# Attention and routed experts on one core: two score rounds for three, weight rows in pairs, a new static order, and a conditional end

## The chip, the cores and the metric

One core of one Trainium2 chip runs the program. The metric is device time in microseconds (us) of one execution; the program reads its inputs from HBM and leaves one output tensor there. Engines are named as in the profile: PE is the matrix engine, PEld its weight loads, DVE the vector engine, ACT the scalar engine, POOL is GpSimd, SP issues transfers.

## The reference

Two layers follow each other. The first is causal attention with a window of 128 positions and a linear distance bias, for 8 batches, 8 heads, 576 positions and a head width of 64. The second sends its 4608 rows of 512 features through a dense two-layer network, and each row also through one of 8 experts of the same size, chosen by the largest gate logit and weighted by its probability.

```python
scores = scale * np.matmul(q, k.transpose(0, 1, 3, 2))
mask = (rel >= 0) & (rel < window)
scores = np.where(mask, scores + bias[None], -1000000000.0)
attn = np.exp(scores - np.max(scores, axis=-1, keepdims=True)); attn = attn / (np.sum(attn, axis=-1, keepdims=True) + 1e-09)
x = np.matmul(attn, v)            # rows of 512: 8 heads side by side
y_dense = np.maximum(x @ w1_dense, 0.0) @ w2_dense
expert_idx = np.argmax(x @ w_gate, axis=1)
y_moe[mask] = gate_w[mask, None] * (np.maximum(x[mask] @ w1[e], 0.0) @ w2[e])
out = y_dense + y_moe
```

The inputs are one fixed draw. Worked out from the reference, the experts get 520, 553, 517, 462, 688, 634, 658 and 576 rows, which is 5, 5, 5, 4, 6, 5, 6 and 5 blocks of 128: 41 blocks.

## The kernel before, in words

The work is cut into 16 units: a batch with four of its eight heads. For a unit, q and k arrive as 128 partitions of 18 rows (`load_qk`), are turned in 32x32 squares by DVE (`turn`, L175), and rounded and put in position order by a copy (`round_qk`, L184), on ACT but for the first q. Scores are made transposed, keys on partitions, in three rounds `pr`, of key blocks (0, 1), (2, 3) and (4): `biases` writes the distance bias into four PSUM banks by 16 matmuls of 32x32 (L404), `scores` adds 16, 16 and 8 matmuls (L422), `expo` takes the exponential of two heads at a time on ACT (L435), `low` makes the low half of the probabilities on DVE (L446; the high half is every second bf16 of the float). The third round has 64 queries, so that its tiles are 128x128 where the others are 128x1024 elements. `attend` multiplies with v (L478) into one PSUM tile of two banks that is freed by `norm` (L496, L497). The result goes to POOL for a row buffer (`row_copy`, L510), and is turned by PE (`flip`, L525) for the gate and the dense layers.

For each batch the gate logits come out of `gate_a`, `gate_av` (DVE adds the two units, L570, L572) and `gate_b` (five matmuls in float, each two instructions, L579); DVE picks the expert (`gate_bv`, L590 to L601), PE counts rows per expert (`gate_c`, L613, which waits for L601), and DVE makes the slot of each row. POOL scatters x rows and dense results into two HBM buffers, ordered by expert (`send_x` L662, `send_y` L750). Weights come in by cast transfers that POOL issues (`load_weights`, L91).

The experts run on blocks of 128 slots. Fifteen whole blocks are taken after five batches (early blocks); the other blocks, always 28 for a total of 43, wait until all rows are scattered (`fetch` L1094 to L1115). A block is four transposes (`turn_x`, L1121), 16 matmuls of 128x128 (`layer1`, L1156), four of 128x512 (`layer2`, L1175), copies by ACT and DVE, and an indirect transfer to the output by POOL (`send_out`, L1199). Rows past an expert's last one are filled by 16 transfers that SP issues near the end, with addresses read from a table (`late_fill`, L1072). Blocks that hold no row then write nothing.

The order of the work on PE, ACT, DVE and SP is written out by hand in three lists of words: `FIRST` (batch 0), `CYCLE` (each of the next batches, `@1` and `@2` being work of one and two batches before) and `LAST` (batch 7 and early blocks). POOL has an order of its own, by `in_turn`. The blocks after the list run in a loop at the end.

Of the kernel before, what the change touches and what calls it, by code (L numbers as in the profile page):

```python
# [23 lines left out]
def kernel(  # L24
# [37 lines left out]
    NL = NB - NE  # L62
    RB = 32
# [108 lines left out]
    def turn(u, nm):  # L172
        t = raw.pop((nm, u))
        s = stg.tile([P, 2, S], F32, name=f"{nm}s", tag=f"{nm}s")
        nc.vector.transpose(out=s.rearrange("p c (r x) -> p r c x", r=R), in_=t)  # L175
        tmp[(nm, u)] = s

    def round_qk(u, nm, copy=nc.scalar.copy):
# [3 lines left out]
        else:  # L182
            d = kTs[u % 2]
        copy(  # L184
            out=d[:, :, 0:S].rearrange("p c (x r) -> p c r x", r=R),
            in_=s.rearrange("p c (r x) -> p c r x", r=R),
# [14 lines left out]
    load_q(0, nc.scalar)  # L201
# [33 lines left out]
    def mask_consts():  # L235
# [11 lines left out]
        for g in range(1, 4):  # L247
            nc.tensor.matmul(
                out=turned[g],
                lhsT=ident2[:, P - 32 * g : 2 * P - 32 * g],  # L250
                rhs=dist,
                start=True,
                stop=True,
            )
# [9 lines left out]
    def mask_rest():  # L264
        for h in range(4, H):
            mask_head(h)

    def more_constants():
        ut_f = ident_x["ut_f"]
        nc.vector.tensor_copy(out=ut_b, in_=ut_f)  # L270
        nc.vector.memset(ones_b, 1.0)

        nc.vector.memset(sel, 0.0)
        for h in range(2):
            nc.vector.tensor_reduce(
                out=sel[64 * h : 64 * h + 64, h, :],
                in_=ident_f.rearrange("p (c x) -> p x c", c=4)[
                    64 * h : 64 * h + 64, 0:E, :
                ],
                op=ALU.add,  # L280
                axis=AX.X,
            )
        for i in range(NT):
            nc.vector.tensor_scalar_add(
                out=tok_c[:, i : i + 1], in0=pidx_f, scalar1=float(i * P)
            )
        nc.vector.tensor_copy(out=em8, in_=em8_i)
        nc.vector.memset(em8[TAIL:P, NT - 1, :], 0.0)
        nc.vector.tensor_copy(out=em8x, in_=em8)
        nc.vector.memset(em8x[TAIL:P, NT - 1, :], 1.0)  # L290
        for i in range(2):
            nc.vector.memset(ohs[i][:, NT, :], 0.0)
        nc.vector.tensor_copy(out=base0, in_=base_i)
        nc.vector.tensor_copy(out=basee, in_=base_i)
        nc.vector.tensor_scalar_mul(out=row_f, in0=pidx_f, scalar1=float(P))
        nc.vector.memset(fill_x, 0.0)
        nc.vector.tensor_copy(out=fill_x.bitcast(I32)[:, TC : TC + 1], in_=oob_f)
# [3 lines left out]
    sel = consts.tile([P, 2, E], F32, name="sel")  # L301
# [14 lines left out]
    def pool_constants():  # L316
# [14 lines left out]
        nc.gpsimd.iota(base_i, pattern=[[ST, E]], base=0, channel_multiplier=0)  # L331
# [13 lines left out]
    def wg_load():  # L345
        nc.sync.dma_start(
            out=wg_pad[:, :, 0:E], in_=moe_w_gate.rearrange("(ds p) e -> p ds e", p=P)
        )
# [22 lines left out]
    lt = dbuf.tile([P, SP_ - DT[1][0] * P], F32, name="ltsb")  # L371
# [11 lines left out]
    def shape(pr):  # L383
        kjs = KP[pr]
        wid = PW if len(kjs) == 2 else TAIL
        return kjs, wid, wid * len(kjs)

    def biases(u, pr):
        hq = u % HQ
        _, _, tot = shape(pr)  # L390
# [957 lines left out]
```

## Time and profile before

| | us |
|---|---|
| median of 3 runs | 369.23 |
| lowest and highest | 366.98 and 371.61 |
| the profiled execution, its own time | 369.47 |
| its span, first to last instruction | 367.8 |
| outside its span | 1.7 |

The profile was taken on one execution. Its rows give, for groups of instructions, the busy time, the mean of one instruction in ns, and the idle time of the engine just before, with what ended it. Matmul ends are modelled, so that a single matmul's mean is longer than its share of the engine; sums over a chain of them are better for that.

### The profile page before, as it was taken

The numbers are of one execution on the slowest core, as the hardware profiler recorded it, in microseconds if no ns is written. First come the engines' busy times: TensorE is split into PE (matmuls) and PEld (weight loads), VectorE is DVE, ScalarE is ACT, GpSimd is POOL, SyncE is SP. The second block draws the span as 40 slices with busy tenths as digits, with TensorE's granted clock in tenths as the row PEclk, the third lists the DMA queues.
The fourth block names the chain that finished last, engine by engine and source line by source line (L and its number), as shares of the span: only waits on it lengthen the run. The fifth ranks groups of instructions, "written<-read, shape, count | busy, mean of one in ns | idle before, by whom it ended". The sixth has DMA issues, their size and how long they took to land.

```text
span 367.8 us, 12624 instructions
## 1 busy us (share of the span) xinstructions
PE 318.5 (87%) x4972; PEld 226.9 (62%) x5003; DVE 273.5 (74%) x487; ACT 272.1 (74%) x430; POOL 223.4 (61%) x245
## 2 busy tenths in 40 slices
PE   3385888987999999999898798999999699999990
PEld 0274565665756756766665675776766467777760
DVE  7867999878799898797996978763645446676660
ACT  5778689897899999799989879876555336555640
POOL 5027612774486786488578768557777535656552
PEclk9999899998999999899999899999999879999997
DMA  7859999289569969949939995798589999989730
GB/s 199 252 132 196 187 237 234 71 234 289 141 138 276 286 131 256 262 109 303 248 107 238 242 260 129 221 255 295 169 303 317 337 303 316 316 279 307 257 123 8
DMA packets 76731, 82.43 MB, mean 224 GB/s; under 512 B 43519, under 2 KB 61311, under 8 KB 76672
## 3 DMA queue, kind: packets, MB, share of 16 engines
q1 hardware_dynamic: 58704, 47.32, 44.7%
q0 software_dynamic: 17680, 33.12, 35.7%
q10 hardware_dynamic: 288, 1.18, 0.9%
q8 instruction: 40, 0.66, 0.8%
q14 instruction: 19, 0.16, 0.1%
HBM read 64.20 MB, written 28.66 MB: 253 GB/s over the span
## 4 chain that ended last, share of the span: by engine, by line
PE 19%; POOL 14%; issue 12%; DVE 9%; ACT 2%; POOLq 1%; DMA 0%; DVEq 0%
POOL out_dram L1199 10%; DVE plo L446 4%; PE yp L733 3%; PE ax L478 3%; PE hp L706 3%; PE hpm L1156 3%; PE y L1175 2%; POOL ys_dram L750 1%; DVE xf L497 1%; POOL xs_dram L662 1%; PE tp L525 1%; DVE qs L175 1%; POOL xrow L510 1%; DVE ks L175 1%; PE xps L1121 1%
## 5 line engine op out<-in xcount | busy, mean ns | idle before, releaser
L446 DVE TENSOR_TENSOR plo<-p 128x1024 bf16<-128x1024 f32 (+1 forms) x96 | 87.1, 929 | 3.6 <-ACT p L435 3.6
L435 ACT ACTIVATE p<-sq 128x1024 f32<-128x1024 f32 (+1 forms) x96 | 74.4, 792 | 9.3 <-PE sq L422 6.8
L478 PEld LDWEIGHTS <-p 128*128 128x128 bf16 (+1 forms) x1152 | 61.9, 105 | 16.3 <-DVE xf L497 8.6
L1199 POOL DMA_INDIRECT out_dram<-yo,xr x43 | 48.4, 1125 | 37.1 <-DVE yo L1187 33.1
L510 POOL CAST xrow<-xf 128x512 bf16<-128x512 f32 (+1 forms) x48 | 47.2, 987 | 38.7 <-DVE xf L497 31.1
L478 PE MATMUL ax<-vf,p 128*128 128x65 bf16 (+1 forms) x576 | 65.2, 203 | 4.6 <-DVE xf L497 4.5
L478 PE MATMUL ax<-vf,plo 128*128 128x65 bf16 (+1 forms) x576 | 64.5, 200 | 1.1 <-DVE plo L446 1.1
L478 PE MATMUL ax<-vl,p 128*128 128x64 bf16 (+1 forms) x576 | 64.7, 199 | 0.0
L662 POOL DMA_INDIRECT xs_dram<-xrow,slot x40 | 46.0, 1150 | 29.1 <-issue 21.3
L750 POOL DMA_INDIRECT ys_dram<-yt,slot x40 | 52.5, 1313 | 15.1 <-ACT yt L745 5.4
L478 PEld LDWEIGHTS <-plo 128*128 128x128 bf16 (+1 forms) x576 | 57.7, 105 | 1.4 <-DVE plo L446 1.3
L1187 DVE SCALAR_TENSOR_TENSOR yo<-y,xr,yr 128x512 f32<-128x512 f32 x43 | 32.1, 750 | 29.1 <-PE y L1175 28.4
L1156 PE MATMUL hpm<-xTm,ws 128*128 128x128 bf16 x688 | 45.7, 221 | 1.1 <-issue 1.0
L1175 PE MATMUL y<-w_all,hTm 128*128 x156 | 43.1, 389 | 0.9
L1156 PEld LDWEIGHTS <-ws 128*128 128x128 bf16 x688 | 41.3, 99 | 3.5 <-issue 1.9
L1168 ACT ACTIVATE hTm<-hpm 128x512 bf16<-128x512 f32 x43 | 25.7, 597 | 23.7 <-PE hpm L1156 22.0
L706 PE MATMUL hp<-xTb,w_all 128*128 128x256 bf16 (+1 forms) x256 | 40.9, 289 | 1.3 <-ACT hTd L721 1.2
L733 PE MATMUL yp<-w_all,hTd 128*128 128x512 bf16 (+1 forms) x145 | 39.0, 381 | 0.7
L184 ACT CAST kT<-ks 128x1152 fp32r<-128x1152 f32 x16 | 37.9, 2370 | 1.9 <-DVE ks L175 1.8
L1130 ACT COPY xTm<-xps 128x512 bf16<-128x512 bf16 x43 | 25.1, 587 | 18.4 <-PE xps L1121 18.3
L1145 DVE COPY ws<-w_all 128x2048 bf16 x43 | 30.1, 703 | 11.3 <-PE hpm L1156 6.5
L497 DVE TENSOR_TENSOR xf<-ax,recip 128x512 f32<-128x512 f32 (+1 forms) x48 | 28.8, 600 | 12.5 <-POOL xrow L510 8.4
(126 smaller groups left out, 538.5 us busy)
## 6 DMA issues: line engine op xcount, KB each, us to landing
yr<-ys_dram SPq DMA_DIRECT2D x43, 256.0 KB
kraw<-in_k_dram SPq DMA_DIRECT2D x16, 576.0 KB
vf<-in_v_dram SPq DMA_DIRECT2D x64, 128.0 KB
w_all<-in_moe_w_dram POOLq DMA_DIRECT2D x16, 512.0 KB, 8.1
qraw<-in_q_dram SPq DMA_DIRECT2D x14, 576.0 KB
xr<-xs_dram SPq DMA_DIRECT2D x43, 130.0 KB
ys_dram<-fill_x SPq DMA_DIRECT2D x8, 256.0 KB
qraw<-in_q_dram ACTq DMA_DIRECT2D x2, 576.0 KB
```

What stands on the lines that cost most here:

```text
L184: copy(out=d[:, :, 0:S].rearrange("p c (x r) -> p c r x", r=R), in_=s.rearrange("p c (r x) -> p c r x", r=R),)
L435: nc.scalar.activation(out=p32, in_=sqs[(u, pr)][i][:, :, 0:tot], func=ACT.Exp, scale=SCALE)
L446: nc.vector.tensor_tensor(out=plo, in0=p32, in1=phi, op=ALU.subtract)
L478: nc.tensor.matmul(out=ax[:rows, i, o0 : o0 + w], lhsT=lhs, rhs=rhs, start=(n == 1), stop=(n == 3 * len(kl)),)
L510: ins = nc.gpsimd.tensor_copy(out=xrows[b % 2].bitcast(BF16)[:rows, qis[0] : qis[0] + nt, hq * 256 : hq * 256 + 256], in_=cur[("xf", u, pr ...
L662: ins = nc.gpsimd.indirect_dma_start(out=xs_dram[:, :], out_offset=bass.IndirectOffsetOnAxis(ap=slots[b][:rows, t : t + 1], axis=0), in_=x ...
L706: nc.tensor.matmul(out=hp[:, 0 : c1 - c0], lhsT=w_all[:, E, 0, kc, c * P : c * P + P], rhs=cur[("xTb", b)][:, kc, c0:c1], start=(kc == 0), ...
L733: nc.tensor.matmul(out=yp[:rows, :], lhsT=cur[("hT", b, hf)][:, c, t0 * P : t0 * P + rows], rhs=w_all[:, E, 1, c, :], start=(c == 0), stop ...
L750: ins = nc.gpsimd.indirect_dma_start(out=ys_dram[:, :], out_offset=bass.IndirectOffsetOnAxis(ap=slots[b][:rows, t : t + 1], axis=0), in_=c ...
L1156: nc.tensor.matmul(out=hp[:, c, :], lhsT=ws[:, kc, c * P : (c + 1) * P], rhs=xT[:, kc, :], start=(kc == 0), stop=(kc == 3),)
L1175: nc.tensor.matmul(out=y, lhsT=hT[:, c, :], rhs=w_all[:, bass.DynSlice(er, 1), 1, c, :], start=(c == 0), stop=(c == 3),)
L1199: ins = nc.gpsimd.indirect_dma_start(out=out[:, :], out_offset=bass.IndirectOffsetOnAxis(ap=xr.bitcast(I32)[:, TC : TC + 1], axis=0), in_= ...
```

## The change

- Scores: two rounds of key blocks (0, 1) and (2, 3, 4). The 64 columns of block 4 take the unused part of block 3's bank, so every round is 128x1024. The last 64 queries of two heads are handled together (`attend_tail`, 18 matmuls where there were 24), in the second half of the PSUM tile of queries 256 to 511, whose `norm` takes the reciprocals of both.
- Turning: DVE's squares are written with two neighbouring rows interleaved, and the copy after it reads in order and writes pairs, where it read single elements 128 bytes apart. The first q is copied by ACT, and loaded by SP.
- Weights: row 256c + 2p + l lies at partition p, so that a partition takes two rows of HBM in one piece. `pick` takes every second column when x or inner features are turned or multiplied.
- Gate: four row blocks side by side (`gate_a` has 10 matmuls), `gate_b` has two matmuls for five, and the first unit's copy is done by ACT.
- Constants of the routing move from DVE to POOL; `xf` has three buffers for two.
- Routing: each expert's region begins with 128 filler rows, written at batch 0 by two transfers (`unused_rows`); `late_fill` goes. Late blocks are counted back from an expert's last row, so that the first of them can overlap an early one; the output transfer of block 15 waits for those of blocks 0 to 14.
- 41 blocks run always; the last two only if more than 26 late blocks are in use, by a register and a branch at the end.
- `FIRST`, `CYCLE` and `LAST` are all new. In `CYCLE`, 4 words stood between `gb` (choice of the expert, DVE) and `pc` (count, PE), none of them PE's; now 23 stand there, 5 of them PE's (`hp` three times, `mask`, `qk`). In `LAST`, `out:12` stands just before `out:15`.

```diff
+    NO = 41
+    def pick(t, c):
+        return t.rearrange("p (c x l) -> p c l x", x=P, l=2)[:, c // 2, c % 2, :]
...
-            out=w_all[:, e, wi, :, :],
-            in_=src.rearrange("(ks p) f -> p ks f", p=P),
+            out=w_all[:, e, wi, :, :].rearrange("p (c l) f -> p c (l f)", l=2),
+            in_=src.rearrange("(c p l) f -> p c (l f)", p=P, l=2),
...
-        nc.vector.transpose(out=s.rearrange("p c (r x) -> p r c x", r=R), in_=t)
+        nc.vector.transpose(
+            out=s.rearrange("p c (a x l) -> p a l c x", x=32, l=2),
+            in_=t.rearrange("p (a l) c x -> p a l c x", l=2),
+        )
...
-            out=d[:, :, 0:S].rearrange("p c (x r) -> p c x r", r=R),
-            in_=s.rearrange("p c (r x) -> p c x r", r=R),
+            out=d[:, :, 0:S].rearrange("p c (x a l) -> p c a x l", x=32, l=2),
+            in_=s.rearrange("p c (a x l) -> p c a x l", x=32, l=2),
...
-    load_q(0, nc.scalar)
+    load_q(0, nc.sync)
...
+    KK = [(0, 1), (2, 3, 4)]
+    def part(kj, odd):
+        c0 = {0: 0, 1: PW, 2: 0, 3: PW, 4: PW + P + TAIL}[kj]
+        if odd and kj >= 2:
+            c0 = 0 if kj == 4 else c0 + TAIL
+        return c0, min(PW, S - kj * P)
...
     def gate_a(u):
+        for t, c in [(t, c) for c in range(2) for t in range(4)] + [(4, 0), (4, 1)]:
+            r0, c0, w = 32 * (t % 4), t // 4 * P, min(P, S - t * P)
...
     def gate_av(u):
+        for r, c0, w in ((P, 0, P), (32, P, TAIL)):
+            src, dst = lp[0:r, c0 : c0 + w], lt[0:r, c0 : c0 + w]
+            if u % HQ == 0:
+                nc.scalar.copy(out=dst, in_=src)
+            else:
+                nc.vector.tensor_tensor(out=dst, in0=dst, in1=src, op=ALU.add)
...
-        for t in range(NT):
+        for t0, t1 in ((0, 4), (4, NT)):
...
-                lhsT=w_all[:, E, 0, kc, c * P : c * P + P],
+                lhsT=pick(w_all[:, E, 0, kc, :], c),
...
+    def unused_rows(b, i):
+        ins = nc.sync.dma_start(
+            out=dst.rearrange("(e s) w -> s e w", e=E)[0:P],
+            in_=src.unsqueeze(1).to_broadcast([P, E, src.shape[1]]),
+        )
...
-    def late_fill():
...
-                in_=xr.bitcast(BF16)[:, kc * P : (kc + 1) * P],
+                in_=pick(xr.bitcast(BF16)[:, 0:DM], kc),
...
-                    lhsT=ws[:, kc, c * P : (c + 1) * P],
+                    lhsT=pick(ws[:, kc, :], c),
...
+        if j == NE:
+            for name in outs:
+                tc.add_manual_dep(
...
+        rest(NO, NO - 3)
+        with tc.If(reg[0] > NO - NE):
+            rest(NB)
```

## Rows read from the trace of the kernel before

**Rows 1.** The page, part 1: busy us, share of the span, instructions
```profile
PE 318.5 (87%) x4972; PEld 226.9 (62%) x5003; DVE 273.5 (74%) x487; ACT 272.1 (74%) x430; POOL 223.4 (61%) x245
```

**Rows 2.** Busy time in five batches, cut at each gate's first DVE operation (L590)
```profile
core 0: us, PE busy (x) PEld busy (x) DVE busy (x) ACT busy (x) POOL busy (x), PEclk, DMA share, GB/s
...
sum 147.40, PE 137.33 PEld 96.12 DVE 126.44 ACT 133.73 POOL 106.09; mean PE 27.47 PEld 19.22 DVE 25.29 ACT 26.75 POOL 21.22
```

**Rows 3.** Busy time by stretch (columns as above): start, late switch, steady blocks
```profile
0.00:10.00 10.00, 3.32 (x19) 0.79 (x19) 7.33 (x28) 5.43 (x6) 5.13 (x32) 1.00 0.78 198
10.00:20.00 10.00, 5.00 (x95) 4.11 (x96) 8.55 (x8) 7.15 (x10) 0.00 (x0) 1.00 0.86 233
20.00:30.00 10.00, 7.43 (x151) 6.26 (x149) 5.30 (x9) 6.76 (x8) 3.43 (x6) 1.00 0.60 131
30.00:40.00 10.00, 6.18 (x121) 4.62 (x118) 8.81 (x13) 8.61 (x11) 7.24 (x4) 0.83 1.15 242
...
290.00:300.00 10.00, 7.25 (x60) 5.14 (x61) 3.96 (x7) 2.11 (x4) 3.35 (x4) 0.66 0.95 306
...
330.00:340.00 10.00, 9.88 (x120) 7.42 (x120) 6.78 (x11) 5.91 (x10) 6.01 (x5) 1.00 0.92 312
```

**Rows 4.** Groups by line and shape: count | busy us, mean ns | idle before
```profile
L435 ACT ACTIVATE p<-sq 128x1024 f32<-128x1024 f32 x64 | 64.6, 1032 | 8.4 <-PE sq L422 6.0 <-PE ax L478 1.5
...
L478 PEld LDWEIGHTS <-p 128*128 128x128 bf16 x896 | 48.9, 104 | 12.4 <-DVE xf L497 8.3 <-issue 3.3
...
L478 PEld LDWEIGHTS <-plo 128*128 128x128 bf16 x448 | 45.2, 103 | 1.4 <-DVE plo L446 1.3
...
L184 ACT CAST kT<-ks 128x1152 fp32r<-128x1152 f32 x16 | 37.9, 2370 | 1.9 <-DVE ks L175 1.8
...
L175 DVE STREAM_TRANSPOSE ks<-kraw 128x1152 f32<-128x1152 f32 x16 | 21.9, 1368 | 3.3 <-DMA kraw<-in_k_dram 3.3
...
L446 DVE TENSOR_TENSOR plo<-p 128x128 bf16<-128x128 f32 x32 | 11.0, 351 | 1.4 <-ACT p L435 1.4
...
L435 ACT ACTIVATE p<-sq 128x128 f32<-128x128 f32 x32 | 9.7, 313 | 0.9 <-PE sq L422 0.8
...
L570 DVE COPY ltsb<-lp 128x320 f32<-128x320 f32 x8 | 3.9, 483 | 1.9 <-PE lp L558 1.9
...
L184 DVE CAST qT<-qs 128x1152 fp32r<-128x1152 f32 x1 | 1.2, 1247 | 0.0
```

**Rows 5.** The chain that ended last: start us, us, what
```profile
235.12 1.21 PE lg L579 x10
...
244.10 1.51 PE ax L478 x48
...
266.20 0.89 PE hpm L1156 x16
...
318.75 1.17 POOL out_dram L1199
...
356.75 0.97 POOL out_dram L1199
```

**Rows 6.** Timeline of PE around 34 us: the third round's bias matmuls
```profile
34.21 0.25 PE L404 MATMUL sq<-mask,ident 32*32 32x64 bf16 x16 [2.56 <-ACT p L435]
```

**Rows 7.** Waits in the five batches of rows 2: us in total, times, longest
```profile
DVE xf L497 <- POOL xrow L510: 7.1, 4, 3.0
PE pc L613 <- DVE oh L601: 7.0, 5, 2.6
```

**Rows 8.** Timelines of SP and PE at the switch to late blocks
```profile
286.52 0.97 SPq L1086 DMA_DIRECT2D ys_dram<-fill_x  x1
288.54 0.37 SPq L1106 DMA_DIRECT2D xr<-xs_dram  x1
...
292.21 0.61 PE L1121 MATMUL xps<-ident,xr 128*128 128x128 bf16 x4 [3.06 <-DMA xr<-xs_dram]
```

**Rows 9.** Line L1199, the output transfers: issue to landing
```profile
DMA to landing us min/median/max: 2.9/4.6/5.8
```

More of the change, by code (lines that the diff above doesn't have):

```diff
@@ L247, in mask_consts @@
         for g in range(1, 4):
[L248 to L254, printed above, removed]
+            o, end = 0, 2 * PW
+            for c0 in (2 * PW - TAIL, 0) if g % 2 else (0,):
+                nc.tensor.matmul(
+                    out=turned[g][:, o : o + end - c0],
+                    lhsT=ident2[:, P - 32 * g : 2 * P - 32 * g],
+                    rhs=dist[:, c0:end],
+                    start=True,
+                    stop=True,
+                    skip_group_check=True,
+                )
+                o, end = o + end - c0, c0
     turned = []
@@ L526, in flip @@
                     out=tp[:, i, c, 0:rows],
[L527 removed]
+                    in_=pick(xf[:rows, i, :], c),
                     identity=ident_f[:rows, :rows],
@@ new lines @@
+        one:0 hTd:0,3@0 turn:3 ex:@0 hm:0 xm:3 pc:@0 cv:@0 hp:0,1@0 gd:@0
+        turn:4 two:1 ws:3 hTd:0,1@0 two:0 ws:5 late:0 yp:1@0 yp:0@0 yt:1@0
+        turn:8 hp:1,0@0 yt:0@0 xm:4 hTd:1,0@0 one:3 hp:1,1@0 turn:6 hp:1,3@0
+        hTd:1,1@0 xs:4@1 xs:0@1 xs:2@1 ys:2@1 ys:3@1 xs:1@1 out:2 yo:1
+        hp:1,2@0 ws:4 one:5 hm:3 hTd:1,2@0 hTd:1,3@0 xs:0@0 xs:4@0 xs:2@0
+        out:1 yo:0 late:1 ys:1@0 out:0 ws:6 two:3 yp:2@0 xm:8 xm:6 hm:5 yp:4@0
+        one:4 two:5 turn:7 one:6 turn:9 yo:3 ws:8 yo:5 late:2 ws:7 yt:4@0
@@ new lines @@
+        yt:2@0 hm:4 hm:6 get:12 get:11 get:14 get:13 two:4 one:8 ws:9 xm:7
+        yo:4 yp:3@0 hm:8 xm:9 one:7 turn:11 two:6 one:9 yt:3@0 turn:10 ws:11
+        yo:6 ys:0@0 xs:1@0 ys:4@0 xs:3@0 ys:2@0 out:3 ws:10 ys:3@0 hm:9 hm:7
+        xm:11 xm:10 out:4 out:5 out:6 two:8 two:9 one:11 turn:12 one:10 hm:11
+        xm:12 yo:8 hm:10 ws:12 ws:13 yo:9 turn:13 turn:14 one:12 two:7 two:11
+        get:16 out:8 get:15 get:17 out:9 yo:7 ws:14 yo:11 xm:13 xm:14 one:13
+        hm:12 two:10 turn:16 one:14 two:12 xm:16 turn:15 ws:15 yo:10 ws:16
@@ L905 @@
+        hm:14 yo:12 hm:13 xm:15 out:7 out:11 two:14 one:16 one:15 two:13 yo:14
+        ws:17 turn:17 yo:13 hm:15 hm:16 xm:17 two:15 out:10 out:14 out:13
+        out:12 yo:15 out:15
     """.split()
@@ L1305, with rest, count @@
         done = {x: 1 + max(k[1] for k in tail if k[0] == x) for x in ("get", *by_block)}
-        while done["get"] < done["two"] + NR:
-            fetch(done["get"])
-            done["get"] += 1
-        for j in range(done["two"], NB):
-            for x, ahead in (("turn", 2), ("xm", 2), ("ws", 2), ("one", 1), ("hm", 1)):
-                if done[x] <= j + ahead < NB:
-                    by_block[x](j + ahead)
-            for x in ("two", "yo", "out"):
-                by_block[x](j)
-            while done["get"] < min(j + NR + 1, NB):
-                fetch(done["get"])
-                done["get"] += 1
+        def rest(end, at=NB):
+            for j in range(done["two"], end):
+                if j == at:
+                    count()
+                while done["get"] < min(j + NR, end):
+                    fetch(done["get"])
+                    done["get"] += 1
+                for x, ahead in (
+                    ("turn", 2),
+                    ("xm", 2),
+                    ("ws", 2),
+                    ("one", 1),
+                    ("hm", 1),
+                    ("two", 0),
+                    ("yo", 0),
+                    ("out", 0),
+                ):
+                    while done[x] <= min(j + ahead, end - 1):
+                        by_block[x](done[x])
+                        done[x] += 1
+        reg = []
+        def count():
+            loads, (n,) = nc.values_load_multi_w_load_instructions(
+                where["n"][0:1, 0:1],
+                min_val=0,
+                max_val=NL,
+                skip_runtime_bounds_check_because="the blocks past the early ones",
+            )
+            for ins in loads:
+                if ins.ins.engine == ENG.Pool:
+                    in_turn(ins)
+            reg.append(n)
+        rest(NO, NO - 3)
+        with tc.If(reg[0] > NO - NE):
+            rest(NB)
 _INS = ['q', 'k', 'v', 'moe_w_gate', 'moe_w1_dense', 'moe_w2_dense', 'moe_w1', 'moe_w2']
```

513 lines of the change are left out of this document (266 added, 247 removed).

## The prediction

> **What bounds the kernel now.** I read the page's busy shares first, then the windows, then the groups by line and shape, then the chain and the waits.
>
> The shares put PE first, at 318.5 us of 367.8, with DVE and ACT at 74% each [rows 1]. The windows tell where this average comes from. Over five batches in the middle, 147.4 us or 29.5 us a batch, the means are PE 27.5, ACT 26.75, DVE 25.3 and POOL 21.2 us [rows 2]. So PE sets the pace there, is idle 2.0 us a batch, and ACT has only 2.7 us to spare: two engines nearly full, which is why small waits can't be absorbed. After the attention PE alone is full: 9.88 of 10 us in a stretch of blocks, with ACT and DVE at 6 to 7 [rows 3]. [...]
>
> The sum below is therefore PE's work plus PE's idle time, stage by stage. It starts at the profiled execution, 369.5 us (367.8 of span and 1.7 around it); the median of the runs, 369.2, is so near that nothing is shifted.
>
> **The change part by part: PE in a batch of attention.** A third round's 16 bias matmuls take 0.25 us [rows 6]; two units give 0.5. The gate's five float matmuls, ten instructions, take 1.21 us in the chain [rows 5], so 0.12 each; four instructions are left, 0.48, and 0.73 goes. The score matmuls keep their columns: nothing. The attention's last 64 queries take 18 matmuls for 24, of which six are two heads wide; at the chain's 31 ns each (48 in 1.51 us [rows 5]) that is between 0.2 us less and as much more; I take 0.1 less. Sum 1.3 us: 27.5 goes to 26.2.
>
> **ACT in a batch.** Four small exponentials of 313 ns go, 1.25 us. The four round copies take 2370 ns for 1152 elements a partition [rows 4]. The exponentials of 128 and 1024 elements, 313 and 1032 ns, give 0.80 ns an element, so an orderly copy of 1152 would take 313 + 1024 x 0.80 = 1.13 us, as an estimate. The copy of before reads single floats 128 bytes apart; the new one reads in order and writes pairs. Its cost lies between 1.13 and 2.37 us; I take 1.25, near the orderly rows, so 4.5 us go. The first unit's two gate copies come to ACT: 2 x 0.31 by the small row. Sum: 26.75 - 1.25 - 4.5 + 0.6 = 21.6 us (between 21.1 and 26.1).
>
> What speaks for and against this from the rows: DVE made one such copy, with the same strided read, in 1247 ns [rows 4], so a strided read as such need not be slow; it is ACT that takes twice its own pace. [...]
>
> **DVE in a batch.** Four small subtractions of 351 ns go, 1.4 us; the gate's two operations of 483 ns [rows 4] become two smaller ones, at most 0.5 together: 25.3 goes to 23.4. The square turns (1368 ns) now write floats 8 bytes apart. No row shows such a write on DVE. Its ends are 1368 and twice that, 5.5 us more a batch and 28.9 in all; I take the lower, as DVE's strided read of 1247 ns for as many elements shows no loss.
>
> **The pace that follows.** PE is the bound at 26.2, with DVE 2.8 and ACT 4.6 us behind. Of PE's 2.0 us idle a batch, 1.4 is one wait: the row count stands right behind the choice of the expert, 7.0 us in five batches [rows 7]. Five words of PE now stand between the two, and that cover hides it; next late is the round trip from exponential to bias, which is shorter by a round. DVE's wait for a free `xf` (7.1 us in five [rows 7]) loses its cause by the third buffer. I leave 0.7 us idle: 26.9 a batch, 2.6 less. Seven batches (the first is in the start): 18 us. Ends: 2.0 idle, 28.2, 9 us less; 0.3 idle, 26.5, 21 us less.
>
> **Start.** Two third rounds go, one of which had PE waiting 2.56 us for ACT [rows 6], and the copies of two units shorten, but the first q's copy moves from DVE (1.25 us) to ACT behind k's. I take 4 us less, between none and 8, of the 18.1 idle. The constants leave DVE, where they stood before the first turn while k was in flight; POOL has no work from 10 to 20 us [rows 3], which covers them: 0. q0 is issued one place later on SP, ahead of v: 0, at worst one SP issue of 0.37 us [rows 8].
>
> **Weights and filler rows.** Half as many pieces for the same weight bytes; no wait of PE on weights stands in these rows, so 0. The filler rows are as many bytes as before, 3.2 MB, moved from the end to the second batch; at the 198 to 242 GB/s of the start that is 13 to 16 us of transfers beside others. I take 0, at worst 3 if loads of v or k come late; DMA was at 0.60 in 20 to 30 us [rows 3].
>
> **Blocks.** The output transfers leave at a steady pitch: 318.75 to 356.75 us is 19 steps of 2.00 us [rows 5]. The fixed draw needs 41 blocks, 26 of them late; the condition is more than 26, so two blocks are skipped: 4.0 us less.
>
> **Switch.** SP's last filler transfer is issued at 286.52, the first late row fetch at 288.54 us, and PE waits until 292.21 [rows 8]. Without 16 fillers in SP's queue, and with the scatters placed ahead of `out:3` to `out:11`, I take 2 us less: between 5 less (the wait and its slow clock gone) and 3 more (order no better).
>
> **Added waits.** Block 15's output transfer waits in POOL's queue for `out:12` to land, 4.6 us [rows 9]; behind it stand the outputs of blocks 16 and on. Four `yo` buffers at 2.0 us cover 8 us; an output takes 1.17 to issue and 4.6 to land, 5.8, so 2.2 us of slack meet 4.6. I take 1.5 us, between 0 and 5. The branch: a register is loaded by each engine three blocks ahead, then each jumps over two blocks while the last output still lands, 4.6 us, which covers it. I take 1 us for what isn't covered, between 0 and 4. [...]
>
> **Sum.** 369.5 - 18 - 4 - 4 - 2 + 1.5 + 1 = 344.0 us.
>
> **The rivals.**
>
> 1. The copies don't get shorter, because pairs written 72 bytes apart cost ACT as much as floats read apart. ACT stays at 26.1 beside PE's 26.2, and two full engines keep the idle 2.0 us: 28.2 a batch, 9 us less for seven; the start gives 1. 369.5 - 9 - 1 - 4 - 2 + 2.5 = 356 us. For: DVE's 1247 shows that the read isn't slow by itself. Against: the pace of all orderly rows on ACT.
> 2. The gain of PE is spent on new waits: the new order lets PE stand 3 us a batch (DVE's turns at twice their time would do that too: 28.9 us of DVE, and 0.7 idle, 29.6 a batch). The batches give nothing, the blocks give 4, the switch 2 and the added waits take 2.5: 366 us. For: nothing in the rows shows the new order. Against: ACT, DVE and POOL all have 2.8 us or more to spare a batch.
> 3. Slower: `pick` makes PE load weights from every second element, 20 loads in a block and 32 in a batch's dense layer, 41 x 20 + 8 x 32 = 1076. If such a load no longer fits beside its matmul, each costs up to the pitch of a 128-column matmul, 56 ns (16 in 0.89 us [rows 5]): 60 us, and 404 us in all. It decides from 30 ns a load, where the sum passes 377. Against: the probabilities' high halves are every second element already, and load in 104 ns where the orderly low halves take 103 [rows 4], both at 31 ns a matmul in the chain.
>
> **How the numbers follow.** The forecast has 0.65, of which 0.03 lies below 331 us, and its own range is 333 to 354. Rival 1 has 0.17, rival 2 0.12, rival 3 0.06. The range of 331 to 362 us holds the forecast but for 0.03 and nearly all of rival 1, and leaves out rivals 2 and 3. Its low end is the sum with the batches at 21, the start at 8 and the switch at 5 us less, with the added waits kept: 334, less 3 for the terms set to 0. Two per cent, about what a measurement of this kernel can tell from no change, is 361.8 and 376.6 us. Faster: the forecast and 0.15 of rival 1, 0.80. Same: rival 2 and the rest of rival 1 but for 0.01, 0.13. Slower: rival 3 and that 0.01, 0.07.
>
> **What would show it.** Right: a pitch of about 27 us between the gates' first operations, PE idle under 1 us a batch, a round copy near 1.25 us, turns still at 1.37, `pc` no longer waiting for `oh`, block pitch still 2.0 with 41 output transfers, ACT near 21.6 us a batch. Wrong: copies at 2.3 us (rival 1); PE idle 3 us or more a batch, or turns over 2 us (rival 2); a block pitch over 2.2 us (rival 3); more than 5 us of idle PE after block 15, or a gap of several us after the last output, would put the loss in the added waits.

## The result, and the profile after

The changed kernel takes 332.48 us (median of 4 runs, 331.73 to 335.06) against 369.62 us for the kernel before beside it. The ratio is 0.9015, with a 95% interval of 0.8950 to 0.9079: faster by about a tenth. The profiled execution took 335.06 us, with a span of 333.4 us and 1.7 us around it.

Two things in the sections above have to be set right first. The copy of `round_qk` before did not read single floats 128 bytes apart, and the diff above prints its two lines otherwise than they stand in the kernel. It reads in order and writes single floats 72 bytes apart; its lines are

```python
out=d[:, :, 0:S].rearrange("p c (x r) -> p c r x", r=R),
in_=s.rearrange("p c (r x) -> p c r x", r=R),
```

The new copy also reads in order, and writes pairs of floats, the pairs 72 bytes apart. So the strided side is the write in both, on ACT and in the one copy that DVE made. Where the prediction says "strided read", read "strided write".

And only one of the two filler transfers leaves near the start. The x rows' filler is issued in the second batch; the larger one, for the dense results, only after the fifth gate:

```profile
46.05 0.56 SPq L834 DMA_DIRECT2D xs_dram<-fill_x  x1
...
180.12 0.45 SPq L834 DMA_DIRECT2D ys_dram<-mask  x1
```

The span became 34.4 us shorter. Cut at the first DVE operation of each batch's gate (L590 before, L655 after), the four parts are these; in the third column stand the prediction's terms, with its seven batches of 2.6 us put where they fall.

| stretch | before, us | after, us | measured | predicted |
|---|---|---|---|---|
| start to second gate | 88.98 | 79.67 | -9.3 | -4 - 2.6 |
| second to seventh gate, five batches | 147.4 | 134.3 | -13.1 | -13.0 |
| seventh gate to the last output's issue | 123.4 | 114.0 | -9.4 | -2.6 - 4 - 2 + 1.5 + 1 |
| last output's issue to the end | 8.0 | 5.4 | -2.6 | 0 |

The page of the kernel after, parts 1 and 3; the second line is POOL's own DMA queue (packets, MB, share), and the third the same queue before.

```profile
PE 302.4 (91%) x4749; PEld 225.8 (68%) x4749; DVE 257.4 (77%) x427; ACT 234.9 (70%) x411; POOL 213.6 (64%) x261
...
q0 software_dynamic: 12912, 34.29, 37.4%
...
q0 software_dynamic: 17680, 33.12, 35.7%
```

Against [rows 1], all engines work less, and PE's share rose from 87% to 91%. The windows of the kernel after say where; columns as in [rows 2], the third column from the end being the granted clock.

```profile
0.00:79.67 79.67, 62.49 (x1092) 48.46 (x1093) 63.54 (x85) 56.70 (x87) 37.35 (x85) 0.91 0.92 220
...
132.14:158.29 26.15, 25.94 (x471) 19.41 (x470) 23.85 (x40) 22.52 (x42) 19.59 (x22) 1.00 0.96 246
158.29:185.99 27.70, 26.45 (x473) 19.49 (x472) 26.68 (x53) 23.16 (x42) 21.00 (x22) 1.00 0.92 251
185.99:213.97 27.98, 26.64 (x480) 19.90 (x479) 23.14 (x40) 22.83 (x42) 20.53 (x21) 1.00 0.84 234
sum 134.30, PE 129.66 PEld 96.74 DVE 121.49 ACT 112.70 POOL 100.05; mean PE 25.93 PEld 19.35 DVE 24.30 ACT 22.54 POOL 20.01
...
213.97:328.02 114.05, 110.28 (x1316) 80.62 (x1313) 72.34 (x135) 65.47 (x125) 75.20 (x73) 1.00 0.85 280
```

In an undisturbed batch PE is busy 25.94 of 26.15 us: hardly anything but PE's own work is left. Over the five batches it is idle 4.64 us, 0.9 a batch, where it was idle 2.0 [rows 2]. The two longer batches carry the routing of the early blocks (53 DVE instructions for 40 in the first) and what follows it. The same cuts in the kernel before:

```profile
0.00:88.98 88.98, 64.45 (x1203) 46.16 (x1205) 73.40 (x121) 70.88 (x94) 41.66 (x71) 0.98 0.86 199
...
88.98:118.39 29.41, 27.41 (x478) 19.50 (x480) 26.10 (x44) 26.56 (x41) 18.20 (x18) 0.94 0.77 198
...
146.79:176.58 29.79, 28.38 (x502) 20.10 (x500) 25.44 (x45) 27.02 (x43) 21.10 (x22) 0.94 0.86 215
...
207.79:236.36 28.57, 26.29 (x437) 18.22 (x440) 22.38 (x41) 25.25 (x42) 21.08 (x23) 0.94 0.81 197
...
236.36:359.78 123.42, 116.73 (x1359) 84.66 (x1378) 73.64 (x140) 67.58 (x129) 74.74 (x72) 0.97 0.85 275
```

The three batches that are shown had a mean granted clock of 0.94 of full speed, and the other two 1.00. In each of the three the granted clock was 0.50 or 0.51 in one stretch of 3.4 us:

```profile
89.80:93.20 3.40, 3.03 (x46) 2.97 (x47) 2.28 (x7) 2.76 (x4) 2.18 (x2) 0.50 1.09 279
...
147.80:151.20 3.40, 3.22 (x47) 3.14 (x48) 2.21 (x6) 2.57 (x4) 3.23 (x4) 0.51 1.09 292
...
209.30:212.70 3.40, 3.40 (x45) 2.99 (x43) 2.27 (x6) 1.98 (x4) 3.12 (x5) 0.50 1.05 321
```

The missing 0.06 of 87.8 us is 5.3 us, as an estimate: up to 1.05 us a batch of what counted as PE's work was the lower clock. The windows can't be compared as they stand, since work slips across the cuts (64 to 96 score matmuls in one window, 80 in a batch). But the 216 attention matmuls that four of them hold take 8.71 and 8.76 us where the mean clock was 0.94, and 7.87 and 8.03 where it was 1.00, and the 20 turns of `flip` 3.65 for 3.16 to 3.19: 1.3 us for these two groups. After, the clock is 1.00 in all five.

The groups of the kernel after by line and shape, as in [rows 4]:

```profile
L1232 PEld LDWEIGHTS <-ws 128*128 128x128 bf16 x656 | 38.9, 98 | 5.0 <-issue 2.0 <-DVE ws L1221 0.2
...
L558 DVE TENSOR_TENSOR xf<-ax,recip 128x512 f32<-128x512 f32 x32 | 22.1, 692 | 3.2
...
L180 DVE STREAM_TRANSPOSE ks<-kraw 128x1152 f32<-128x1152 f32 x16 | 21.9, 1367 | 2.7 <-ACT p L436 1.4 <-DMA kraw<-in_k_dram 1.3
...
L192 ACT CAST kT<-ks 128x1152 fp32r<-128x1152 f32 x16 | 20.3, 1269 | 0.7 <-DVE ks L180 0.6
L588 PEld LDWEIGHTS tp<-ident_f,xf 128*128 128x128 f32 x128 | 17.9, 208 | 8.0 <-issue 3.2 <-ACT p L436 1.3 <-DVE xf L558 1.2
...
L678 PE MATMUL pc<-oh,ones_b 128*128 128x40 bf16 x8 | 1.5, 192 | 0.0
```

The reader is to see five things: the copy at 1269 ns for 2370; the turns unchanged at 1367, although they now write floats 8 bytes apart; the weight loads of every second bf16 at 98 ns; the float ones of `flip` (L588) at 208 ns, for which `pick` was new too; and `pc` and `xf` without the waits of [rows 7] (0.0 for `pc`, none on POOL for `xf`).

The chain that ended last, as in [rows 5]:

```profile
285.99 1.18 POOL out_dram L1275
...
320.16 1.18 POOL out_dram L1275
```

These are 17 steps of 2.01 us: the pitch of the late blocks did not change, and with 41 outputs two steps are saved.

### The profile page after: what moved, and what is told of

It reads as the page before. It is cut to its first block, busy times and chain, and to the rows that moved or that the text cites. A ratio compares the mean times of both kernels' runs of the same rounds, so it can differ in the third digit from the quotient of the medians.

```text
span 333.4 us, 12007 instructions
## 1 busy us (share of the span) xinstructions
PE 302.4 (91%) x4749; PEld 225.8 (68%) x4749; DVE 257.4 (77%) x427; ACT 234.9 (70%) x411; POOL 213.6 (64%) x261
## 3 DMA queue, kind: packets, MB, share of 16 engines
q0 software_dynamic: 12912, 34.29, 37.4%
## 4 chain that ended last, share of the span: by engine, by line
PE 43%; DVE 19%; ACT 14%; issue 9%; POOL 8%; DMA 3%; SPq 1%; POOLq 1%; DVEq 0%; ACTq 0%
POOL out_dram L1275 8%; DVE plo L448 7%; PE ax L539 7%; PE yp L800 6%; PE hp L771 6%; ACT p L436 5%; PE tp L588 5%; PE sq L425 4%; PE hpm L1232 4%; PE y L1251 3%; DVE ks L180 3%; PE lp L621 3%; DVE xf L558 2%; DVE vl L202 2%; PE ax L490 2%
## 5 line engine op out<-in xcount | busy, mean ns | idle before, releaser
L448 DVE TENSOR_TENSOR plo<-p 128x1024 bf16<-128x1024 f32 x64 | 79.4, 1247 | 8.2 <-ACT p L436 7.3
L436 ACT ACTIVATE p<-sq 128x1024 f32<-128x1024 f32 x64 | 64.1, 1031 | 6.4 <-PE sq L425 3.2
L1275 POOL DMA_INDIRECT out_dram<-yo,xr x41 | 47.2, 1151 | 28.2 <-DVE yo L1263 20.5
L539 PEld LDWEIGHTS <-p 128*128 128x128 bf16 x896 | 47.4, 101 | 6.8 <-DVE xf L506 3.9
L539 PE MATMUL ax<-vf,p 128*128 128x65 bf16 x448 | 48.0, 199 | 2.9 <-DVE xf L506 1.9
L539 PE MATMUL ax<-vf,plo 128*128 128x65 bf16 x448 | 47.6, 196 | 0.4 <-DVE plo L448 0.4
L539 PE MATMUL ax<-vl,p 128*128 128x64 bf16 x448 | 47.8, 196 | 0.0
L539 PEld LDWEIGHTS <-plo 128*128 128x128 bf16 x448 | 43.7, 100 | 0.6 <-DVE plo L448 0.6
L800 PE MATMUL yp<-w_all,hTd 128*128 128x512 bf16 x160 | 39.8, 379 | 1.1 <-ACT xT L609 0.6
L609 ACT COPY xT<-tp 128x512 f32<-128x512 f32 (+1 forms) x48 | 23.5, 489 | 20.2 <-PE tp L588 20.1
L588 PE MATMUL tp<-ident_f,xf 128*128 128x128 f32 (+1 forms) x160 | 30.9, 309 | 5.3 <-DVE xf L558 3.5
```

Source lines behind the costliest of these rows:

```text
L436: nc.scalar.activation(out=p32.rearrange("p (g c) -> p g c", g=2), in_=sqs[(u, pr)][i], func=ACT.Exp, scale=SCALE,)
L448: nc.vector.tensor_tensor(out=plo, in0=p32, in1=phi, op=ALU.subtract)
L539: nc.tensor.matmul(out=ax[:rows, i, o0 : o0 + w], lhsT=lhs, rhs=rhs, start=(n == 1), stop=(n == 3 * len(kl)),)
L588: nc.tensor.transpose(out=tp[:, i, c, 0:rows], in_=pick(xf[:rows, i, :], c), identity=ident_f[:rows, :rows],)
L800: nc.tensor.matmul(out=yp, lhsT=cur[("hT", b, hf)][:, c, c0 : c0 + P], rhs=w_all[:, E, 1, c, :], start=(c == 0), stop=(c == 3),)
L1275: ins = nc.gpsimd.indirect_dma_start(out=out[:, :], out_offset=bass.IndirectOffsetOnAxis(ap=xr.bitcast(I32)[:, TC : TC + 1], axis=0), in_= ...
```

## The experiments

Each was run beside the kernel before, and is compared by its ratio to it. The experiments were run in three groups, and the changed kernel itself was run in each group as a yardstick. In the first group, with the old copy, the near count and the old rows:

> The changed kernel once more, as the yardstick for the runs beside it. Every theory expects 332 to 335 us, a ratio to the kernel before near 0.90, gates 26 us apart.

It took 335.39 us, ratio 0.9132 [0.9015, 0.9248], with gates 26.15 us apart in undisturbed batches, as above. In the second group, with 41 blocks, 43 blocks and the late fillers:

> The changed kernel once more, as the yardstick beside e4, e5 and e7: 332 to 336 us.

336.39 us, ratio 0.9014 [0.8869, 0.9158]. In the third group, with the kernel before with the new copy, the turn in order and the first q:

> The changed kernel once more, as the yardstick beside e2, e8 and e10: 332 to 336 us.

369.20 us, ratio 0.9419 [0.9356, 0.9482]: throughout this last group every kernel, the one before too (393.65 us), took some 25 to 35 us longer, for a reason that no run shows, so that its times stand only beside each other.

### The old copy in the new kernel

```diff
-        nc.vector.transpose(
-            out=s.rearrange("p c (a x l) -> p a l c x", x=32, l=2),
-            in_=t.rearrange("p (a l) c x -> p a l c x", l=2),
-        )
+        nc.vector.transpose(out=s.rearrange("p c (r x) -> p r c x", r=R), in_=t)
...
-            out=d[:, :, 0:S].rearrange("p c (x a l) -> p c a x l", x=32, l=2),
-            in_=s.rearrange("p c (a x l) -> p c a x l", x=32, l=2),
+            out=d[:, :, 0:S].rearrange("p c (x r) -> p c r x", r=R),
+            in_=s.rearrange("p c (r x) -> p c r x", r=R),
```

> The changed kernel with the old turn and the old round copy: DVE writes its squares in order, ACT writes single floats 72 bytes apart; all else stays. Theory (ACT was the second full engine): the copy goes back from 1.28 to 2.37 us, ACT from 22.5 to 26.9 us a batch, above PE's 25.9, so the gates stand 27 to 28.5 us apart and the time is 7 to 16 us longer, 340 to 349 us. Rival (PE's work and the order made the gain, ACT had room anyway): the copy is 2.37 but the gates stay under 26.7 us apart and the time is under 337 us.

359.38 us, ratio 0.9767 [0.9643, 0.9892]: 24.0 us longer than the yardstick. The loss was larger than the theory's: between the profiled executions, the five batches lost 15.2 us, which the theory allows, but another 12.0 were lost before the second gate. Its groups, its windows (five batches, cut at the gates) and its waits in them (us in total, times, longest):

```profile
L189 ACT CAST kT<-ks 128x1152 fp32r<-128x1152 f32 x16 | 37.6, 2350 | 0.2 <-DVE ks L180 0.2
```

```profile
sum 150.70, PE 131.53 PEld 98.73 DVE 122.32 ACT 132.33 POOL 105.51; mean PE 26.31 PEld 19.75 DVE 24.46 ACT 26.47 POOL 21.10
```

```profile
PEld sq L422 <- ACT qT L189: 8.2, 5, 1.7
...
PE sq L422 <- ACT qT L189: 5.9, 5, 1.2
```

A batch takes 30.1 us, more than before the change (29.5), though PE's work is 26.3 and ACT is busy for 26.5 only. So the theory had the wrong mechanism: it isn't a full ACT that costs. PE is idle 3.8 us a batch, and the waits say for what: for the 1.1 us more that each copy lasts on the way from a load to PE's next scores, and for what queues behind it on ACT. The timelines of ACT and PE show one such wait:

```profile
171.24 2.38 ACT L189 CAST qT<-qs 128x1152 fp32r<-128x1152 f32 x1
```

```profile
173.68 0.74 PE L422 MATMUL sq<-qT,kT 32*128 32x256 f32 x16 [1.22 <-ACT qT L189]
```

In each undisturbed batch PE also waits 0.77 and 0.56 us for `hTd` and 0.99 us for `yt`, both made by ACT. The new order has room for copies of 1.27 us and none for copies of 2.35; lengths between were not tried. Where the 2.3% that are left come from can be read off too: against the kernel before, the second gate comes at 88.7 us for 89.0 and the five batches take 3.3 us longer, but 10.6 us are gained from the seventh gate to the last output, where the two blocks fewer are, and 2.7 behind it. With long copies the new order gives nothing in the attention.

### The new copy in the kernel before

The same four lines, exchanged in the kernel before and nothing else.

> The kernel before with the new turn and the new copy alone: DVE writes its squares in pairs, ACT copies pairs. Theory (the copies are most of the gain, but only where they stand on PE's path: the old order keeps them ahead of their use, and its other stalls, the row count's above all, stay): copies 1.28 us, ACT 22.4 us a batch, PE idle still 1.5 us or more, gates 28 to 29 us apart, time 4 to 12 us shorter than before, 358 to 366 us. Rival (the old kernel was held up by ACT as the changed one with old copies is): 20 us or more shorter, under 350 us. Rival (the old order is cut to the long copy and gains nothing): within 3 us of before.

390.91 us, ratio 0.9971 [0.9923, 1.0018]: no gain that can be told, though the copies shortened, where the whole change gave 5.8% in this slower third group. Since even the changed kernel's undisturbed batches took 28.3 us in it, a small gain could be hidden. Groups:

```profile
L187 ACT CAST kT<-ks 128x1152 fp32r<-128x1152 f32 x16 | 20.7, 1295 | 2.0 <-DVE ks L175 2.0
...
L616 PE MATMUL pc<-oh,ones_b 128*128 128x40 bf16 x8 | 1.5, 192 | 3.7 <-DVE oh L604 3.6
...
L187 DVE CAST qT<-qs 128x1152 fp32r<-128x1152 f32 x1 | 0.8, 761 | 0.0
```

The last row is the copy that DVE makes here: 761 ns where the same copy took 1247 [rows 4]. And `pc` still waits. Copy and order each need the other: short copies in the old order gave 0.3% of the 5.8% of their group, the rest of the change with long copies 2.3% of the 8.7% of its group.

### The count right behind the choice of the expert

```diff
-        gb:@1 hp:0,0@1 w:1@1 xs:0@2 exp:1,0,0@0 mask:1,1@0 ys:4@2 yt:3@2
+        gb:@1 pc:@1 hp:0,0@1 w:1@1 xs:0@2 exp:1,0,0@0 mask:1,1@0 ys:4@2 yt:3@2
...
-        norm:0,2@0 exp:1,1,0@0 pc:@1
+        norm:0,2@0 exp:1,1,0@0
```

> The changed kernel with the word of the row count (pc) in the repeated list put straight behind the choice of the expert (gb), as in the kernel before. Theory (the wait of PE for DVE's choice was the largest stall a batch, 1.4 us and the slow clock behind it): PE waits 1 to 2.6 us there in each of six or seven batches, time 6 to 16 us longer, 339 to 349 us. Rival (with ACT and DVE no longer full, PE finds the choice made sooner, or makes the loss good from the words around it): under 3 us longer.

338.21 us, ratio 0.9191 [0.9052, 0.9329]: 2.8 us longer, with overlapping intervals, so that the time tells little and the waits have to. The gates are 27.3 us apart, 1.1 more. PE's timeline:

```profile
161.61 0.27 PE L678 MATMUL pc<-oh,ones_b 128*128 128x40 bf16 x5
...
164.27 0.60 PE L771 MATMUL hp<-xTb,w_all 128*128 128x256 bf16 x4 [0.83 <-ACT hTd L786]
```

Even there `pc` waits only once in eight batches, 1.2 us; what PE waits for now is the dense layer's `hTd`, as its words come earlier. So it wasn't the cover behind the choice that took the wait away: from the logits to the count PE has 1.5 us of other work here (0.8 at the one gate where it waits), and had 1.6 before. DVE's and PE's timelines of the kernel before, around one gate, show what the wait was:

```profile
144.56 2.32 DVE L446 TENSOR_TENSOR plo<-p 128x1024 bf16<-128x1024 f32 x2
146.79 0.20 DVE L590 TENSOR_REDUCE mx<-lg 128x5 f32<-128x40 f32 x1
```

```profile
144.14 1.28 PE L579 MATMUL lg<-sel,ltsb 128*128 128x8 f32 x10
...
147.98 0.30 PE L613 MATMUL pc<-oh,ones_b 128*128 128x40 bf16 x5 [1.01 <-DVE oh L601]
```

The logits were there at 145.4, and PE had 1.6 us of other work before the count, but DVE had two low halves ahead of the choice and began it at 146.8. In the kernel after, DVE is there first and waits 0.18 us for the logits:

```profile
158.29 0.20 DVE L655 TENSOR_REDUCE mx<-lg 128x5 f32<-128x40 f32 x1 [0.18 <-PE lg L644]
```

The other gates say the same. At the five gates of [rows 7], DVE began the choice 2.93, 0.64, 1.37, 1.35 and 2.64 us after the last logit, each time behind the same two low halves, and PE waited 2.57, 0.28, 1.01, 0.99 and 2.15 us: each wait is that lateness less 0.4 to 0.5 us. In the kernel after and in this experiment DVE begins at most 0.5 us after the logits at these gates.

### The weight rows in the old layout

```diff
-        return t.rearrange("p (c x l) -> p c l x", x=P, l=2)[:, c // 2, c % 2, :]
+        return t[:, c * P : (c + 1) * P]
...
-            out=w_all[:, e, wi, :, :].rearrange("p (c l) f -> p c (l f)", l=2),
-            in_=src.rearrange("(c p l) f -> p c (l f)", p=P, l=2),
+            out=w_all[:, e, wi, :, :],
+            in_=src.rearrange("(ks p) f -> p ks f", p=P),
```

The gate's weights go back likewise.

> The changed kernel with the old weight rows: row 128c + p at partition p, and x and inner features turned in order instead of in steps of two; all else stays. Theory (the pairs of rows touch only transfers, which PE does not wait for, and a weight load from every second element costs nothing): within 1.5 us of the changed kernel, weight loads 98 to 100 ns in both. Rival (fewer and longer pieces relieve the transfers, which are 0.9 to 1.0 busy in the batches): 3 to 8 us longer, with later landings and new waits for data.

337.75 us, ratio 0.9121 [0.8903, 0.9339]: not to be told from the yardstick. But two opposite effects lie in it. Groups, windows (two undisturbed batches) and part 3 of its page:

```profile
L586 PEld LDWEIGHTS tp<-ident_f,xf 128*128 128x128 f32 x128 | 13.8, 143 | 8.3 <-issue 3.0 <-ACT p L434 1.6 <-DVE xf L556 1.2
```

```profile
sum 51.55, PE 50.80 PEld 37.58 DVE 47.87 ACT 44.87 POOL 38.91; mean PE 25.40 PEld 18.79 DVE 23.94 ACT 22.43 POOL 19.46
```

```profile
q0 software_dynamic: 17520, 34.29, 39.2%
```

The float loads of the turn take 143 ns again, PE's work in a batch is 25.40 us for 25.93, and the gates are 25.8 us apart for 26.15. Against that, the end is longer: POOL's timeline has the last output at

```profile
328.49 0.98 POOL L1273 DMA_INDIRECT out_dram<-yo,xr  x1 [1.53 <-DMA out_dram<-yo,xr]
```

and the span ends at 336.1, 7.6 us later, where the yardstick has 5.4. What lasts there is a DRAIN, an instruction of POOL's sequencer at the end of the program. Its rows give min, median and max in ns, here before, after, and with the old rows; the span ends 0.8 to 0.9 us behind the longest one:

```profile
L1343 POOLq DRAIN  x3: 46/111/7677, 359.3 to 367.5; - x3
...
L1462 POOLq DRAIN  x3: 46/109/4719, 327.8 to 333.1; - x3
...
L1460 POOLq DRAIN  x3: 46/109/7006, 328.3 to 335.8; - x3
```

Of the edits to the new kernel, this one alone brought the long end back.

### Pairs, but the turn in order

Here the turn and the gate read x in order, so that the gate's weights and the dense network's first layer keep the old rows; all other weights stay in pairs.

```diff
-                    in_=pick(xf[:rows, i, :], c),
+                    in_=xf[:rows, i, c * P : c * P + P],
...
+        if i == 0:
+            ins = nc.gpsimd.dma_start(
+                out=w_all[:, e, wi, :, :], in_=src.rearrange("(ks p) f -> p ks f", p=P)
+            )
```

> The changed kernel with PE's turn of the attention result (floats) in order again, and with it the gate weights and the dense layer's first weight in old rows; the experts' weights stay in pairs, x of the blocks and inner features are turned in steps of two. Theory (a float weight load from every second element is slow, 208 ns where the kernel with old rows has 143, and PE is full, so it costs 0.35 us a batch): loads near 143 ns, gates 25.8 us apart where they were 26.15, 2 to 3 us shorter than the changed kernel. Rival (the load is hidden beside the matmul before it): no difference over 1 us.

366.33 us, ratio 0.9355 [0.9293, 0.9417], in the slower third group: 0.7%, 2.9 us, less than the yardstick there, with intervals that overlap by about half their width. Its groups, its windows at the start, and those of the yardstick of the same group:

```profile
L591 PEld LDWEIGHTS tp<-ident_f,xf 128*128 128x128 f32 x128 | 13.8, 143 | 12.2 <-issue 7.2 <-ACT hTd L789 2.1 <-DVE xf L561 1.2
```

```profile
0.00:40.00 40.00, 23.46 (x451) 17.57 (x451) 29.71 (x37) 26.99 (x39) 17.67 (x65) 1.00 0.95 214
```

```profile
0.00:40.00 40.00, 25.10 (x428) 19.36 (x429) 27.54 (x34) 25.04 (x36) 17.73 (x65) 0.96 0.89 205
```

PE's loads are short again, and the end stays at 5.4 us. Its lead stands already at the first gate (40.8 against 43.6 us), where the clock was 1.00 against 0.96, and executions of the changed kernel differ by 2.0 us there (42.2 to 44.2). The later batches took 28.2 us in both, so that the theory's shorter pitch did not show in this group. It is a candidate to beat both kernels, not one that is shown to.

### Without the branch, and with 43 blocks

```diff
-        rest(NO, NO - 3)
-        with tc.If(reg[0] > NO - NE):
-            rest(NB)
+        rest(NO)
```

> The changed kernel with 41 blocks and no register, no condition and no code for the last two blocks; for other inputs than the fixed draw it would leave rows out. Theory (the branch is covered, apart from what its queues do at the end): 0 to 1.5 us shorter. [...]

332.53 us, ratio 0.8979 [0.8888, 0.9069]: 0.4%, some 1.3 us, shorter than the kernel with the branch, within the uncertainty. POOL issues its last two outputs 1.29 us apart, where with the branch they are 1.95 apart (326.07 and 328.02 us) and the last waits for an earlier output transfer. POOL's timeline:

```profile
324.77 0.98 POOL L1275 DMA_INDIRECT out_dram<-yo,xr  x1 [0.77 <-DVE yo L1263]
326.06 0.98 POOL L1275 DMA_INDIRECT out_dram<-yo,xr  x1 [0.31 <-issue]
```

With `rest(NB)` in that place, all 43 blocks run:

> The changed kernel with all 43 blocks run always, no condition. Theory A (two blocks cost two steps of the pitch): 4.0 us longer than e4. Theory B (two blocks without rows also lengthen the end: in the kernel before, 8.0 us pass from the start of the last output transfer to the end of the span, in the changed kernel 5.4): 6 to 7 us longer than e4, with 7 to 8 us after the last output transfer.

339.82 us, ratio 0.9147 [0.9028, 0.9266]: 6.2 us more than with 41 by the ratios, 4.9 by the fastest runs of each, for two blocks at a pitch of 2.0 us, 4.0; with these intervals neither is told from 4.0. The end after the last output is 5.5 us, for 5.3 with 41: fewer blocks hardly shorten it.

### The filler rows late again

The two filler transfers, `pad:0` and `pad:1` of `FIRST`, moved to a place in `LAST` before the first late fetch: they are issued at 252.4 and 252.9 us, where the kernel after issues them at 46.1 and 180.1. The line of `LAST`:

```diff
-        yo:6 ys:0@0 xs:1@0 ys:4@0 xs:3@0 ys:2@0 out:3 ws:10 ys:3@0 hm:9 hm:7
+        yo:6 ys:0@0 xs:1@0 ys:4@0 xs:3@0 ys:2@0 out:3 ws:10 ys:3@0 pad:0@0 pad:1@0 hm:9 hm:7
```

> The changed kernel with the two filler transfers moved from batch 0 to the place before the first late fetch, where the kernel before filled; they are the same bytes, in two transfers instead of 16. Theory (3.2 MB of filler in front of the late fetches made a part of the wait at the switch to late blocks): PE waits 3 us or more before block 15 and the time is 4 to 9 us longer. Rival (the new order of scatters and outputs alone mended the switch): under 2 us longer.

337.18 us, ratio 0.9093 [0.9000, 0.9186]: 0.9%, 2.9 us, longer than the yardstick, with overlapping intervals. In the profiled execution, the longest of the four (341.33 us), PE's timeline has two new waits, and the clock falls behind them (mean 0.86 from 255 to 280 us):

```profile
265.31 1.21 PE L1234 MATMUL hpm<-xTm,ws 128*128 128x128 bf16 x16 [2.82 <-issue]
...
275.58 0.40 PE L1199 MATMUL xps<-ident,xr 128*128 128x128 bf16 x4 [2.08 <-DMA xr<-xs_dram]
```

This lies between theory and rival. The two waits, 4.9 us together, stand in no execution with early fillers that was profiled; that the late fillers were a part of the old wait at the switch is likely by that, and its size is not shown.

### The first q from ACT's queue

```diff
-    load_q(0, nc.sync)
+    load_q(0, nc.scalar)
```

> The changed kernel with the first q loaded from ACT's queue again, beside k's on SP's. Theory (k alone arrives sooner: 5.0 us where it was 6.6): the first turn starts at 6.4 to 6.7 us, the first exponential 1 us later, and 0.5 to 1.5 us of it stay in the total. Rival (v and the rest of the start set the first batch's end): no difference over 0.5 us in the first gate or the time.

370.89 us, ratio 0.9506 [0.9427, 0.9586], 0.9% more than the yardstick of that group, intervals overlapping. DVE's first turn begins at 6.63 us for 5.43, PE's first scores at 11.59 for 10.39, and the first gate comes at 44.2 for 43.6. So SP's queue is worth 1.2 us at the first scores; what is left at the gate is less than the 2.0 us by which executions of the changed kernel differ there.

## Why the prediction was right, and where it wasn't

**Direction and size.** 344.0 us was forecast, with 331 to 362; it was 332.5, and 335.1 in the profiled execution. So the median lies near the low end of the range, and just below the forecast's own range of 333 to 354. The mechanism of the batches held in the main, and the terms of the start and of the end were too small: 2.7 us at the start, 3.3 behind the seventh gate, and 2.6 at the very end, together 8.6 of the 8.9 us between 344.0 and 335.1.

**The pitch.** 26.9 us was predicted and 26.86 measured, with other parts than predicted. PE's work was to fall from 27.5 by 1.3 us. It fell by 1.5, of which up to 1.05 is the clock that no longer drops, so that as little as 0.5 is work that went. Line by line, what was priced came out near its size: in us a batch, the bias matmuls went from 2.24 to 1.74, `gate_b` from 1.28 to 0.59, and the attention's matmuls, at full clock, from 7.9 to 7.7. The scores, put at nothing, went from 3.6 to 3.2. What was not priced took some of it back: `gate_a` rose from 1.49 to 1.70, and `flip`, at full clock, from 3.2 to 3.8. The prediction's sum left `flip` out, which `pick` also touches; with its float loads in order PE's work is 25.40, another 0.53 less. PE's idle time fell to 0.9 a batch, where I left 0.7. That the pitch came out to 0.04 us is thus partly luck: the clock, which the sum did not price, made up for the work that stayed.

**Where the idle time was.** I put it to the cover between choice and count. The wait went, as said, but by another mechanism, and the cover wasn't needed: DVE had begun the choice late, behind two low halves, and in the new order it doesn't. The wait may also have cost more than its 7.0 us: the clock's three stretches at 0.50 begin at 89.8, 147.8 and 209.3 us, and PE had been idle for `oh` by 2.6, 1.0 and 2.2 us until 90.2, 148.0 and 209.0. At the other two gates it was idle by 1.0 and 0.3 us, and the mean clock of the batch was 1.00. Whether the 5.3 us of lower clock follow from this wait, no run shows: a wait of 1.0 us stands on both sides.

**ACT and the copies.** The copy was taken at 1.25 us and takes 1.27 to 1.29; ACT was to be 21.6 us a batch and is 22.5; the rest of that difference was not followed. Writing pairs shortened it on ACT (2370 to 1269 ns) and, other than I argued, on DVE too (1247 to 761 ns): DVE's row was no evidence that a strided access costs nothing, since I had nothing orderly to hold it against. The float weight loads of `flip`, with every second float, take 208 ns where in order they take 143. Why pairs of floats shorten the one and steps of two lengthen the other, no run shows.

**DVE.** 23.4 was predicted, 24.3 is the mean, 23.85 in an undisturbed batch. The turns keep 1.37 us, the lower end that I took. `xf`'s wait is gone; the third buffer wasn't tried alone.

**Start.** -4 was taken, of the 18.1 us that PE is idle in the first 40 us of [rows 3]; -6.7 is left of the -9.3 when one batch's 2.6 is taken off. PE's idle time up to the second gate fell from 24.5 to 17.2 us. With the old copies the first gate comes 4.6 us later (46.8 for 42.2 in the same group) and the second 12.0 later (88.7 for 76.8), about where it came before the change (89.0), a part of it by the clock, whose mean there was 0.90 for 0.98: without the short copies nothing of this gain is left, and I had given them a part of 4 us. And I priced one wait on a third round, 2.56 [rows 6]; the timeline before has a second one:

```profile
18.00 0.28 PE L404 MATMUL sq<-mask,ident 32*32 32x64 bf16 x16 [2.06 <-ACT p L435]
```

The first k also landed earlier, as the first turn begins at 5.05 us for 6.64; that q0's place on SP, put at 0, does this is shown by the experiment that gives it back to ACT's queue. Against this the clock: its mean up to the second gate was 0.91 in this execution, 0.98 before.

**Blocks.** Two steps of 2.0 us, as said.

**Switch.** 2 us less was taken from a range of 5 less to 3 more; the slow clock that it speaks of is the mean of 0.66 from 290 to 300 us in [rows 3]. PE's idle time from the seventh gate to the last output fell from 6.7 to 3.8 us, 2.9, and the clock there rose from 0.97 to 1.00, 3.7 of 123.4 us: with the blocks' 4.0 that makes 10.6, for 9.4 us that went. Of the 9.4, 4.0 are the blocks and, by the table's split, 2.6 one batch; with the 2.1 us of added waits below counted back, some 4.9 are left for the switch, as an estimate, near the low end of the range. The late fillers may be 2.9 us of it.

**Filler rows.** 13 to 16 us of transfers were put into the second batch and priced at 0. Only about a third of the bytes leave there, at 46.05 us, and the rest at 180.12; so the term was not tried as it stands.

**Added waits.** 1.5 us for the output of block 15: PE idles 0.77 us before that block's first layer, as PE's timeline has it,

```profile
272.36 2.25 PE L1232 MATMUL hpm<-xTm,ws 128*128 128x128 bf16 x32 [0.77 <-PE y L1251]
```

which the row puts to PE's own `y`, so that the output's part of it is not shown; and 1 us for the branch, which measured about 1.3, within the uncertainty.

**The end.** Nothing was said of the time after the last output. It is 8.0, 8.0 and 7.6 us in the three kernels whose weights all come in by the old rows (POOL's queue with 17,520 or 17,680 packets), and 5.3 to 5.5 in all the others (12,912 to 13,168). The experiment with the old rows shows that the rows cause it, and that it is POOL's DRAIN that lasts (7.01 us for 4.72); whether it is the number of packets that sets it, no run shows by itself. I wrote "half as many pieces for the same weight bytes; so 0", and looked for what it costs only at PE's waits.

**The rivals.** The first fell by its condition, as the copies did shorten; its price of 356 us was near the 359 that long copies cost, but by luck: it had a pitch of 28.2 us where 30.1 was measured. The second fell: PE stands 0.9 us a batch, not 3. The third holds for bf16 not at all (98 ns), for floats it does: 208 ns a load where 143 would do, on the 20 loads a batch that the list of 1076 left out.

## What to carry to other kernels

When a consumer waits, look first at where the producer's own queue stood when its input was ready: here the added cover behind the producer was not needed, and its place in its own queue was what counted. Test the parts of a change by taking each out of the new kernel, not only by adding it to the old: here neither the copy nor the order shows more than a small part of its worth without the other. And an edit that looks neutral in the total can be a loss and a gain at two places; the busy time of one undisturbed batch and the time after the last output show both.

## What the runs showed of the hardware that was not expected

- The weight loads of `flip` took 208 ns with every second float and 143 to 149 ns with floats in order; those of `layer1`, in bf16, took 98 ns with every second element and 99 in order.
- The copies that write single floats 72 bytes apart take 1.6 times (DVE, 1247 and 761 ns) to 1.9 times (ACT, 2370 and 1269 ns) as long as those that write pairs.
- The time from the last output to the end went with the packets of POOL's own queue over the whole program: 7.6 to 8.0 us with some 17,600, 5.3 to 5.5 with some 13,000. The longest DRAIN of POOL's sequencer fills most of it: 7.68 us before, 4.72 after.
